# Attention decode step with a gated MLP on one core: the last head group's softmax between its predecessor's value chunks, the output projection around the last values, and one MLP weight in two transfers

## The chip, the core and the metric

The kernel runs on one core of a Trainium2 chip. The core has a matrix engine (TensorE, PE in the profile), a vector engine (VectorE, DVE), a scalar engine (ScalarE, ACT), GpSimd (POOL) and SyncE (SP), which here only issues transfers from HBM to the on-chip memory. Each engine runs its own queue of instructions in order, and the engines wait for one another and for transfers through semaphores. The metric is the device time of one execution in microseconds (us). The time before is the median of three runs.

## What is computed

One token of a pre-norm transformer block: attention against a cache of 4096 positions with 32 heads of 128, then a gated MLP with a tanh GELU. All inputs are bf16.

```python
def _A_ref(x, k_cache, v_cache, wq, wo):      # 32 heads, each with its own K and V
    q = (x @ wq).reshape(B, Sq, Hq, Dh)...
    scores = jnp.einsum("bhqd,bhkd->bhqk", q, k) * (Dh ** -0.5)
    p = _softmax(scores, axis=-1)
    o = jnp.einsum("bhqk,bhkd->bhqd", p, v)
    return o.reshape(B, Sq, Hq * Dh) @ wo

def _B_ref(x, w_gate, w_up, w_down):          # 640 -> 1728 -> 640
    h = _gelu(x @ w_gate) * (x @ w_up)
    return h @ w_down

h = x + _A_ref(_layernorm(x), k_cache, v_cache, wq, wo)
out = h + _B_ref(_layernorm(h), w_gate, w_up, w_down)
```

K and V are 32 MB each, and all that is read comes to 84 MB.

## The kernel before

The 32 heads are worked in 8 groups of 4 (`NG = 8`, numbered 0 to 7). A group's K and V fill one buffer each, of which there are two (`kbuf`, `vbuf`), so group g can be loaded when group g - 2 is done with its buffer. Partitions hold head and position: 32 partitions for each head, 128 positions in each partition.

The order of the instructions on each engine is written out by hand: a small scheduler class records each operation with the operations that it waits for, in program order, and each engine executes its own in that order. So a step that is written earlier stands earlier in the queue of its engine, and an operation that waits holds up all that stands behind it on its engine.

For one group the steps are small functions, and the loop over n interleaves those of three groups:

- `mult` (DVE, L321): K times the query, in four pieces; `fold` (PE, L330): eight matmuls with the identity for each piece, which add up parts of each product; `red` (DVE, L337): the rest of the sum, giving the scores.
- `top` (DVE, L345): the maximum of each partition. `turn` (PE, L349): these maxima turned into one row. `head` (DVE, L354): one maximum for each head. `soft` (PE L359, then ACT L362 and L366): the maximum spread to all partitions, and four exponentials, one for each head.
- `values` (PE, L377): 32 matmuls of 512 columns, in four chunks of 8. The first three chunks of group n - 1 stand in iteration n, the last in iteration n + 1. For the last group `values_last` (L385) does the same with 128 matmuls of 4 columns, with V as the stationary operand.
- `extract` (DVE, L391 and L394) and `column` (PE, L399): a group's result taken out of the accumulator and turned into a column for each head.

Every two groups (a quarter w of the heads, 8 heads) are finished together: `total` (PE, L403) and `invert` (DVE, L425) give the reciprocal sums of the softmax, `spread` (DVE, L410 and L412), `gather` (PE, L417) and `place` (DVE, L421) scale the result and put it into the form that the output projection reads. `project` (PE, L551) multiplies one quarter with its part of wo, in 40 matmuls of one column each.

After the loop there is a tail. Before the change it stands in this order: the last group's last reduction, `top`, `place` of quarter 2, `turn`, `head`, the last value chunk of group 6, `soft`, `extract` and `column` of group 6, `total` and `invert` of quarter 3; then `project` of quarters 0, 1 and 2; then the last group's values; then `spread`, `gather`, `place` and `project` of quarter 3. The residual and the layer norm follow (L563 to L286), then 70 matmuls with w_gate and 70 with w_up (`up`, L591), the GELU and its product with the up part (DVE, the last step `hm` in L607), a small matmul for the uneven remainder (L609), 56 matmuls with w_down (L623), a copy (L627) and the store (L628).

All large transfers are issued by SP in one queue. Behind the loop these are: wo's first three quarters, the last V in two parts (the first three quarters of the positions, then the last), wo's last quarter, w_gate, w_up, and w_down in four parts (80, 1280, 640 and 160 KB). w_gate and w_up are written over the two K buffers, w_down over a V buffer, wo over wq. So w_up waits for the last `mult`, and w_down for the last value chunk of group 6. w_gate and w_up have five slices each (`c` in `up`), and each slice's 14 matmuls wait for the transfer that brings it.

Of the kernel before, what the change touches and what calls it, by code (L numbers as in the profile page):

```python
# [23 lines left out]
NG = H // HG  # L24
# [3 lines left out]
NP = R // RP  # L28
# [81 lines left out]
def bass_sequential_preLN__gqa_block_cached__glu_gated_geglu__decode_kernel(  # L110
# [129 lines left out]
    kfree, vfree = [None] * NG, [None] * NG  # L240
# [78 lines left out]
    def mult(g, s):  # L319
        n = g * NP + s  # L320
        return S.op("vector", lambda v: v.tensor_tensor(  # L321
            out=prod[n % NPR][:, :, :], in0=kbuf[g % 2][:, s * RP:(s + 1) * RP, :],
            in1=qb[:, g, :].unsqueeze(1).to_broadcast([128, RP, DH]), op=ALU.mult),
            [d_k[g], t_qb[g], fold_done.get(n - NPR)])

    def fold(g, s, t_mult):
        n = g * NP + s
        W = 512 // RP
        for j in range(DH // W):
            fold_done[n] = S.op("tensor", lambda t, j=j: t.matmul(  # L330
                pf[n % 2][:, :], Ibf[:, :], prod[n % NPR][:, :, j * W:(j + 1) * W],
                start=(j == 0), stop=(j == DH // W - 1)),
                [t_mult, t_ibf, red_done.get(n - 2)], token=(j == DH // W - 1))

    def red(g, s):
        n = g * NP + s
        red_done[n] = S.op("vector", lambda v: v.reduce_sum(  # L337
            sc[g % 2][:, s * RP:(s + 1) * RP],
            pf[n % 2][:, :].rearrange("p (r w) -> p r w", r=RP), axis=AX.X),
            [fold_done[n], t_exp[g - 2] if g >= 2 else None])  # L340
# [3 lines left out]
    def top(g):  # L344
        t_mx[g] = S.op("vector", lambda v: v.reduce_max(  # L345
            mx[:, g:g + 1], sc[g % 2][:, :], axis=AX.X), [red_done[g * NP + NP - 1]])

    def turn(g):
        t_mm[g] = S.op("tensor", lambda t: t.matmul(  # L349
            pm[0:1, 0:128], mx[:, g:g + 1], I32[:, :], start=True, stop=True),  # L350
            [t_mx[g], t_i32, t_exp[g - 1] if g else None])

    def head(g):
        t_mr[g] = S.op("vector", lambda v: v.reduce_max(  # L354
            mrow[0:1, g * HG:(g + 1) * HG],
            pm[0:1, 0:128].rearrange("p (h q) -> p h q", h=HG), axis=AX.X), [t_mm[g]])

    def soft(g):
        d = S.op("tensor", lambda t: t.matmul(  # L359
            pm[:, 256:256 + HG], ones[0:1, :], mrow[0:1, g * HG:(g + 1) * HG],  # L360
            start=True, stop=True), [t_mr[g]])
        e = S.op("scalar", lambda a: a.activation(  # L362
            nb[:, g * HG:(g + 1) * HG], pm[:, 256:256 + HG], ACTF.Copy, scale=-SCALE), [d])
        for hh in range(HG):
            lo, hi, h = hh * PPH, (hh + 1) * PPH, g * HG + hh
            t_exp[g] = S.op("scalar", lambda a, lo=lo, hi=hi, h=h, hh=hh: a.activation(  # L366
                P4[g % 2][lo:hi, :, hh], sc[g % 2][lo:hi, :], ACTF.Exp,
                bias=nb[lo:hi, h:h + 1], scale=SCALE, accum_out=RS[lo:hi, h:h + 1]),
                [e, t_p4[g % 2], t_rs, t_pv[g - 2] if g >= 2 else None])
# [3 lines left out]
    def values(g, lo, hi):  # L373
        for i in range(lo, hi):
            r = i * VR
            last = i == NV - 1
            t_pv[g] = S.op("tensor", lambda t, i=i, r=r, last=last: t.matmul(  # L377
                pv[g % 2][0:VM, :], P4[g % 2][:, r:r + VR, :], vbuf[g % 2][:, r:r + VR, :],
                start=(i == 0), stop=last),
                [t_exp[g], d_v[g][r], t_ext[g - 2] if g >= 2 else None], token=last)  # L380
        vfree[g] = t_pv[g]

    def values_last(g):
        for r in range(R):
            t_pv[g] = S.op("tensor", lambda t, r=r: t.matmul(  # L385
                pq[:, 0:HG], vbuf[g % 2][:, r, :], P4[g % 2][:, r, :],
                start=(r == 0), stop=(r == R - 1)),
                [t_exp[g], d_v[g][r], t_qb[NG - 1]], token=(r == R - 1))
# [9 lines left out]
    def column(g):  # L398
        t_acc[g] = S.op("tensor", lambda t: t.matmul(  # L399
            po[:, g * HG:(g + 1) * HG], xz[g % 2][:, :], hsel[:, :], start=True, stop=True), [t_ext[g]])  # L400

    def total(w):
        t_zz[0] = S.op("tensor", lambda t: t.matmul(  # L403
            pz[:, 0:HW], ones[:, :], RS[:, w * HW:(w + 1) * HW], start=True, stop=True),
            [t_exp[2 * w + 1], t_aP[w - 1] if w else None])

    def spread(w, src):
        for ps, lo, n, tok in src:
            h0 = w * HW + lo
            a = S.op("vector", lambda v, ps=ps, h0=h0, n=n: v.tensor_mul(  # L410
                aT[:, h0:h0 + n], ps, rz[:, h0:h0 + n]), [t_rz[w], tok])
        t_aL[0] = S.op("vector", lambda v: v.tensor_tensor(  # L412
            out=aL[:, :, :], in0=aT[:, w * HW:(w + 1) * HW].unsqueeze(2).to_broadcast([128, HW, DJ]),
            in1=jmask[:, :].unsqueeze(1).to_broadcast([128, HW, DJ]), op=ALU.mult), [a, t_jm, t_aP[w - 1] if w else None])
# [5 lines left out]
    def place(w, b):  # L420
        t_aP[w] = S.op("vector", lambda v: v.tensor_copy(  # L421
            aP[:, w * HW:(w + 1) * HW], pz[:, 16:16 + HW]), [b])

    def invert(w):
        t_rz[w] = S.op("vector", lambda v: v.reciprocal(  # L425
            rz[:, w * HW:(w + 1) * HW], pz[:, 0:HW]), [t_zz[0]])
# [7 lines left out]
    for n in range(NG):  # L434
        w = (n - 3) // 2 if n >= 3 and n % 2 else None
        p, o = n - 1, n - 2

        t_mul[0] = mult(n, 0)
        if p >= 0:
            red(p, NP - 1)  # L440
            top(p)
        if w is None and n >= 4:
            place((n - 4) // 2, t_g)
        t_mul[1] = mult(n, 1)

        fold(n, 0, t_mul[0])
        if p >= 0:
            turn(p)
            head(p)
        if o >= 0:  # L450
            values(o, 3 * CH, NV)
        fold(n, 1, t_mul[1])
        red(n, 0)
        t_mul[2] = mult(n, 2)
        if p >= 0:
            soft(p)
        if w is not None:
            total(w)
        if 2 <= n + 1 < NG:
            t_qlast = query(n + 1)  # L460
        fold(n, 2, t_mul[2])
        red(n, 1)
        if w is not None:
            invert(w)
        if o >= 0:
            extract(o)
        t_mul[3] = kfree[n] = mult(n, 3)
        if o >= 0:
            column(o)
        if p >= 0:  # L470
            values(p, 0, CH)
        fold(n, 3, t_mul[3])
        red(n, 2)
        if w is not None:
            spread(w, [(po[:, w * HW:(w + 1) * HW], 0, HW, t_acc[o])])
        if p >= 0:
            values(p, CH, 2 * CH)
        if w is not None:
            t_g = gather(w)
        if p >= 0:  # L480
            values(p, 2 * CH, 3 * CH)

        if n == 0:
            load_k(2)
            load_v(1)
        else:
            if 2 <= n < NG - 1:
                load_v(n)
            if n + 2 < NG:
                load_k(n + 2)  # L490


    g = NG - 1
    w = NW - 1


    red(g, NP - 1)
    top(g)
    place(w - 1, t_g)
    turn(g)  # L500
    head(g)
    values(g - 1, 3 * CH, NV)
    soft(g)
    extract(g - 1)
    column(g - 1)
    total(w)
    invert(w)

    def pieces(slot, dst, src, cuts, waits):
        toks = []  # L510
# [7 lines left out]
    def load_wo(lo, hi):  # L518
# [8 lines left out]
    d_wg = pieces("wg", wg_sb, B_w_gate[:, :].rearrange("(p c) n -> p c n", c=NC_D),  # L527
                  [0, 5], [kfree[NG - 2]])
    d_wu = pieces("wu", wu_sb, B_w_up[:, :].rearrange("(p c) n -> p c n", c=NC_D),
                  [0, 5], [kfree[NG - 1]])  # L530
    d_wdr = S.dma("sync", "wdr", lambda s: s.dma_start(
        wd_sb[:, NFT, 0:D // 2], B_w_down[NFT * 128:DF, :].rearrange("r (h n) -> (r h) n", h=2)), [vfree[NG - 2]])
    d_wd = []
# [11 lines left out]
    def project(w):  # L545
        tok = None
        for c in range(HW):
            for cc in range(NC_D):
                last = w == NW - 1 and c == HW - 1 and cc == NC_D - 1
                first = w == 0 and c == 0 and cc == 0  # L550
                tok = S.op("tensor", lambda t, c=c, cc=cc, first=first, last=last: t.matmul(  # L551
                    pp[:, cc:cc + 1], wo_sb[:, w, c, cc::NC_D], aP[:, w * HW + c:w * HW + c + 1],
                    start=first, stop=last, skip_group_check=True),
                    [t_aP[w], d_wo[w], red_done[NG * NP - 2]], token=last)
        return tok

    for i in range(w):
        project(i)
    values_last(g)
    spread(w, [(po[:, w * HW:w * HW + HG], 0, HG, t_acc[NG - 2]), (pq[:, 0:HG], HG, HG, t_pv[NG - 1])])  # L560
    place(w, gather(w))
    b = project(w)
# [99 lines left out]
```

## Time and profile before

| | |
|---|---|
| median of 3 runs | 205.08 us (204.92 to 206.71) |
| the profiled execution | 206.38 us, of which the span from the first to the last instruction is 205.1 us |
| granted TensorE clock, mean over the span | 0.907 |
| PE busy | 158.6 us (77%), 1069 matmuls |
| DVE busy | 116.8 us (57%) |
| ACT busy | 30.4 us (15%) |
| read from HBM | 84.23 MB, 411 GB/s over the span |

The profile is one execution on the chip. Busy times are shares of the span; transfers and engines run beside one another, so the shares do not add up. In the chain of waits and in the timeline each line has the start, the length, the engine and the line of the program, all in us from the first instruction. The time from issue to landing of a transfer includes its wait in the queue behind the ones before it.

### The profile page before, as it was taken

The page shows a single profiled execution, that of the slowest core. Times are in us where ns is not written, and L with a number is a line of the kernel's source. Part 1 is how long each engine was busy: PE and PEld are TensorE (multiplying, and loading weights), DVE is VectorE, ACT ScalarE, POOL GpSimd, SP SyncE. Part 2 cuts the span into 40 slices and gives each one's busy share as a digit, 9 for nine tenths or more (in the row PEclk, how much of TensorE's full clock was granted, in tenths as well). Part 3 has the DMA queues.
Part 4 walks back from the last instruction along what each step waited for, and adds up shares of the span by engine and source line. Part 5 has one row for each costly group of instructions (what it writes and reads, how often), then busy time and mean ns, then how long its engine had stood idle before and what let it go on. Part 6 is the DMA issues. An engine that isn't in the chain of part 4 may idle for free.

```text
span 205.1 us, 2478 instructions
## 1 busy us (share of the span) xinstructions
PE 158.6 (77%) x1069; PEld 73.7 (36%) x1075; DVE 116.8 (57%) x152; ACT 30.4 (15%) x110; POOL 1.2 (1%) x7
## 2 busy tenths in 40 slices
PE   0002759679869968998999499999986999597595
PEld 0001113233324322443343124334422434397494
DVE  4004087997099538875991777599719782401221
ACT  2000210006003200330060004102400130400000
POOL 1000000000000000000000000000000000000000
PEclk9999999999999996999999759999997899965555
DMA  7999999999999999999999999999999999999980
GB/s 256 407 455 409 415 460 454 409 415 447 457 409 422 428 474 409 412 417 466 434 415 422 434 457 415 415 422 460 441 412 422 402 423 454 402 431 428 412 329 0
DMA packets 4162, 84.38 MB, mean 411 GB/s; under 512 B 568, under 2 KB 824, under 8 KB 952
## 3 DMA queue, kind: packets, MB, share of 16 engines
q1 hardware_dynamic: 4008, 84.23, 96.2%
q8 instruction: 8, 0.13, 0.3%
q10 hardware_dynamic: 144, 0.00, 0.0%
q14 instruction: 2, 0.02, 0.0%
HBM read 84.23 MB, written 0.00 MB: 411 GB/s over the span
## 4 chain that ended last, share of the span: by engine, by line
DMA 43%; PE 31%; DVE 19%; ACT 4%; issue 2%; DVEq 0%
DMA kbuf<-in_A_k_cache_dram 36%; DVE prod L321 13%; PE pf L330 10%; DMA x_sb<-in_A_x_dram 8%; PE pu L377 4%; PE pg L377 4%; PE pf L551 3%; DVE sc L337 3%; PE pq L300 2%; ACT P L366 2%; PE pq L385 2%; PE pg L591 2%; PE pu L591 2%; DVE xz L394 1%; PE pf L623 1%
## 5 line engine op out<-in xcount | busy, mean ns | idle before, releaser
L321 DVE TENSOR_TENSOR prod<-kbuf,qb 128x4096 bf16<-128x4096 bf16 x32 | 72.8, 2279 | 36.6 <-DMA kbuf<-in_A_k_cache_dram 30.4
L330 PE MATMUL pf<-prod,Ibf 128*128 128x512 bf16 x256 | 66.7, 408 | 17.2 <-DVE prod L321 17.2
L330 PEld LDWEIGHTS pf<-prod,Ibf 128*128 128x128 bf16 x256 | 24.4, 103 | 56.4 <-DVE prod L321 23.7
L377 PE MATMUL pg<-vbuf,P 128*16 128x512 bf16 x128 | 30.1, 379 | 0.1
L337 DVE TENSOR_REDUCE sc<-pf 128x32 f32<-128x512 f32 x32 | 21.7, 678 | 6.2 <-PE pf L330 6.2
L377 PE MATMUL pu<-vbuf,P 128*16 128x512 bf16 x96 | 24.5, 407 | 0.0
L362 ACT ACTIVATE nb<-pm 128x4 f32<-128x4 f32 x8 | 1.4, 173 | 123.9 <-PE pm L359 123.9
L366 ACT ACTIVATE P<-sc,nb 32x128 bf16<-32x128 f32 x32 | 18.5, 578 | 0.9
L377 PEld LDWEIGHTS pg<-vbuf,P 128*16 128x16 bf16 x128 | 10.6, 89 | 14.9 <-issue 1.7
L272 PE MATMUL pz<-st,ones 128*128 128x2 f32 x4 | 1.2, 364 | 17.6 <-DVE st L271 17.6
L300 PE MATMUL pq<-wq_sb,xb 128*128 128x512 bf16 x34 | 10.8, 452 | 4.2 <-DVE xb L286 2.2
L377 PEld LDWEIGHTS pu<-vbuf,P 128*16 128x16 bf16 x96 | 8.8, 96 | 13.5 <-issue 4.5
L306 ACT CAST qb<-pq 32x128 bf16<-32x128 f32 x32 | 8.2, 256 | 6.5 <-PE pq L300 5.8
L366 ACT ACTIVATION_READ_ACCUMULATOR P<-sc,nb 32x1 f32 x32 | 8.0, 251 | 0.0
L551 PE MATMUL pf<-aP,wo_sb 128*128 128x1 bf16 x160 | 6.8, 178 | 1.1 <-issue 0.8
L289 DVE CAST x<-x_sb 128x5 f32<-128x5 bf16 x1 | 0.2, 172 | 12.9 <-DMA x_sb<-in_A_x_dram 12.9
L272 PEld LDWEIGHTS pz<-st,ones 128*128 128x128 f32 x4 | 1.0, 313 | 17.6 <-DVE st L271 17.6
L394 DVE TENSOR_REDUCE xz<-xm 16x128 f32<-16x512 f32 x7 | 7.2, 1023 | 0.2
L551 PEld LDWEIGHTS pf<-aP,wo_sb 128*128 128x128 bf16 x160 | 6.7, 131 | 1.2 <-issue 0.8
L300 PEld LDWEIGHTS pq<-wq_sb,xb 128*128 128x128 bf16 x40 | 3.8, 111 | 8.2 <-DVE xb L286 2.3
L283 ACT ACTIVATE ln<-ln 128x1 f32<-128x1 f32 x2 | 0.4, 202 | 30.7 <-DVE ln L281 30.7
L410 DVE TENSOR_TENSOR aT<-pq,rz 128x4 bf16<-128x4 f32 x1 | 0.2, 161 | 8.0 <-PE pq L385 8.0
(77 smaller groups left out, 69.4 us busy)
## 6 DMA issues: line engine op xcount, KB each, us to landing
kbuf<-in_A_k_cache_dram SPq DMA_DIRECT2D x8, 4096.0 KB, 25.2
vbuf<-in_A_v_cache_dram SPq DMA_DIRECT2D x7, 4096.0 KB, 22.7
wq_sb<-in_A_wq_dram SPq DMA_DIRECT2D x1, 5120.0 KB, 15.3
wo_sb<-in_A_wo_dram SPq DMA_DIRECT2D x1, 3840.0 KB, 28.4
vbuf<-in_A_v_cache_dram SPq DMA_DIRECT2D x1, 3072.0 KB, 18.3
wg_sb<-in_B_w_gate_dram SPq DMA_DIRECT2D x1, 2160.0 KB, 27.7
wu_sb<-in_B_w_up_dram SPq DMA_DIRECT2D x1, 2160.0 KB, 27.7
wo_sb<-in_A_wo_dram SPq DMA_DIRECT2D x1, 1280.0 KB, 23.0
```

Source lines behind the costliest of these rows:

```text
L272: c = S.op("tensor", lambda t: t.matmul(ps[:, 0:2], ones[:, :], st[:, o:o + 2], start=True, stop=True), [b, t_one])
L300: tok = S.op("tensor", lambda t, c=c, n0=n0: t.matmul(pq[:, :], xb[:, c, :], wq_sb[:, c, n0:n0 + HG * DH], start=(c == 0), stop=(c == NC_D ...
L306: t_qb[g] = S.op("scalar", lambda a, lo=lo, hi=hi, hh=hh: a.copy(qb[lo:hi, g, :], pq[lo:hi, hh * DH:(hh + 1) * DH]), [tok])
L321: return S.op("vector", lambda v: v.tensor_tensor(out=prod[n % NPR][:, :, :], in0=kbuf[g % 2][:, s * RP:(s + 1) * RP, :], in1=qb[:, g, :]. ...
L330: fold_done[n] = S.op("tensor", lambda t, j=j: t.matmul(pf[n % 2][:, :], Ibf[:, :], prod[n % NPR][:, :, j * W:(j + 1) * W], start=(j == 0) ...
L337: red_done[n] = S.op("vector", lambda v: v.reduce_sum(sc[g % 2][:, s * RP:(s + 1) * RP], pf[n % 2][:, :].rearrange("p (r w) -> p r w", r=R ...
L366: t_exp[g] = S.op("scalar", lambda a, lo=lo, hi=hi, h=h, hh=hh: a.activation(P4[g % 2][lo:hi, :, hh], sc[g % 2][lo:hi, :], ACTF.Exp, bias= ...
L377: t_pv[g] = S.op("tensor", lambda t, i=i, r=r, last=last: t.matmul(pv[g % 2][0:VM, :], P4[g % 2][:, r:r + VR, :], vbuf[g % 2][:, r:r + VR, :],
L385: t_pv[g] = S.op("tensor", lambda t, r=r: t.matmul(pq[:, 0:HG], vbuf[g % 2][:, r, :], P4[g % 2][:, r, :], start=(r == 0), stop=(r == R - 1 ...
L394: t_ext[g] = S.op("vector", lambda v: v.reduce_sum(xz[g % 2][:, :], xm[:, :, :].rearrange("p r d -> p d r"), axis=AX.X), [a, t_acc[g - 2] ...
L551: tok = S.op("tensor", lambda t, c=c, cc=cc, first=first, last=last: t.matmul(pp[:, cc:cc + 1], wo_sb[:, w, c, cc::NC_D], aP[:, w * HW + c ...
L591: b = S.op("tensor", lambda t, s=s, c=c, part=part, first=first, last=last: t.matmul(ps[:, s:s + 1], part, hln[:, c:c + 1], start=first, s ...
```

## The change

There are three edits, all near the end of the program.

1. The last group's last `red`, its `top`, `turn` and `head` stand in the loop's last iteration, between the second and the third value chunk of group 6, ahead of `gather` of quarter 2. `soft` of the last group stands ahead of the fourth chunk, and `place` of quarter 2 behind `head`.
2. `project` of quarters 0 and 1 comes directly behind the fourth chunk; `column` of group 6 and `total` and `invert` of quarter 3 come behind these projections; then the last group's values, and behind them `project` of quarter 2. Then `spread`, `gather`, `place` and `project` of quarter 3 as before.
3. w_up is loaded in two transfers, slices 0 to 2 (1296 KB) and slices 3 and 4 (864 KB), with a semaphore each.

No instruction is added or removed on PE, DVE and ACT; SP has one transfer more.

```diff
             spread(w, [(po[:, w * HW:(w + 1) * HW], 0, HW, t_acc[o])])
         if p >= 0:
             values(p, CH, 2 * CH)
+        if n == NG - 1:
+            red(n, NP - 1)
+            top(n)
+            turn(n)
+            head(n)
         if w is not None:
             t_g = gather(w)
...
-    red(g, NP - 1)
-    top(g)
     place(w - 1, t_g)
-    turn(g)
-    head(g)
+    soft(g)
     values(g - 1, 3 * CH, NV)
-    soft(g)
     extract(g - 1)
-    column(g - 1)
-    total(w)
-    invert(w)
...
     d_wu = pieces("wu", wu_sb, B_w_up[:, :].rearrange("(p c) n -> p c n", c=NC_D),
-                  [0, 5], [kfree[NG - 1]])
+                  [0, 3, 5], [kfree[NG - 1]])
...
-    for i in range(w):
+    for i in range(w - 1):
         project(i)
+    column(g - 1)
+    total(w)
+    invert(w)
     values_last(g)
+    project(w - 1)
     spread(w, [(po[:, w * HW:w * HW + HG], 0, HG, t_acc[NG - 2]), (pq[:, 0:HG], HG, HG, t_pv[NG - 1])])
     place(w, gather(w))
     b = project(w)
```

## The prediction

> **What bounds the kernel now.** I read the page first (busy shares, slices, transfers), then the chain of waits, then the timeline from 158 us, because the edits touch nothing earlier. The chain, in order of time (start, us, what):
>
> ```profile
> 175.27 0.32 PE pm L359 x2
> 175.59 0.02 issue
> ...
> 178.26 0.39 PE pz L403 x2
> 178.65 4.78 PE pf L551 x120
> 183.43 0.86 PE pq L385 x32
> ...
> 188.09 1.36 PE pf L551 x30
> 189.45 0.80 issue
> 190.25 0.54 PE pf L551 x10
> ...
> 193.57 3.58 PE pg L591 x70
> 197.15 3.43 PE pu L591 x70
> ...
> 201.09 2.00 PE pf L623 x30
> ```
>
> From 175.59 the tail is a serial run on PE: a hole to 178.26 while ACT makes the last exponentials, 120 projections, the last values, 40 more projections, the layer norm, gate, up, down. No wait in it ends with a transfer. But the transfers run just ahead of it. Their issues in the timeline, and the time from issue to landing in the list of transfers:
>
> ```profile
> 161.02 0.81 SPq L252 DMA_DIRECT2D vbuf<-in_A_v_cache_dram  x2
> ...
> 161.88 0.43 SPq L519 DMA_DIRECT2D wo_sb<-in_A_wo_dram  x1
> ...
> 162.36 0.43 SPq L513 DMA_DIRECT2D wg_sb<-in_B_w_gate_dram  x1
> ...
> 167.53 0.33 SPq L513 DMA_DIRECT2D wu_sb<-in_B_w_up_dram  x1
> ...
> 175.67 1.38 SPq L536 DMA_DIRECT2D wd_sb<-in_B_w_down_dram  x3
> ```
> ```profile
> wg_sb<-in_B_w_gate_dram SPq DMA_DIRECT2D x1, 2160.0 KB, 27.7
> wu_sb<-in_B_w_up_dram SPq DMA_DIRECT2D x1, 2160.0 KB, 27.7
> wo_sb<-in_A_wo_dram SPq DMA_DIRECT2D x1, 1280.0 KB, 23.0
> wd_sb<-in_B_w_down_dram SPq DMA_DIRECT2D x1, 1280.0 KB, 22.8
> ...
> wd_sb<-in_B_w_down_dram SPq DMA_DIRECT2D x1, 640.0 KB, 23.9
> wd_sb<-in_B_w_down_dram SPq DMA_DIRECT2D x1, 160.0 KB, 23.8
> ```
>
> Issue plus landing: last values 179.32 and 181.80 (the second issue at 161.40, with 20.4 us), last quarter of wo 184.88, w_gate 190.06, w_up 195.23; w_down's three issues lie 0.475 apart, so 198.47, 200.04, 200.42. All go through one queue and the 16 DMA engines are 9 tenths busy until 200. So there are two limits: PE's tail, now 203.08, and the last w_down landing, 200.42, which no edit of PE's order moves. What the change can win is the distance between them, less the matmuls that must follow the landing.
>
> **The change, part by part, on the clock of this profile.**
>
> *Softmax between the value chunks.* The last reduction and `top` end on DVE at 170.61 already (L345: 170.32 + 0.29), but `turn` stood behind another chunk and ran at 173.32. Now it follows chunk 2 (end 171.39): 0.22, gather 0.11, chunk 3 1.82, so `soft` starts at 173.54 and the exponentials end at 173.86 + 0.20 + 4 x 0.605 = 176.5 instead of 178.22. PE blocks at `turn` if the maximum is late (gather and chunk 3 queue behind): slack 0.78. It blocks at `soft` if `head` is late (chunk 4 queues behind): `head` ends near 171.9, slack 1.6. Both free; if that cover were gone, each late us is a us on PE. `place` now stands behind `head` on DVE; only the projection of quarter 2 reads it, 11 us later. Chunk 4 ends 0.32 later, at 175.59, behind `soft`; `extract` and the w_down issues, which wait for that chunk, start 0.32 later. The issues are covered by 20 us of queued transfers (w_up lands at 195.2); without that cover they would cost 0.32.
>
> *Projections into the hole.* From 175.59 PE runs 80 projections at 4.78/120 = 0.0398: 178.78. `column` and `total` (0.38 + 0.39) to 179.55; what they need (xz at 177.4, exponentials at 176.5) is there, and `invert` follows on DVE beside the values. The last values take 187.07 - 183.43 = 3.64, to 183.19. Their data: 179.32 is just in time, and matmul 97 starts near 182.28, after 181.80. So the last values end 3.88 earlier than before.
>
> *Quarter 2 behind the values.* 40 x 0.0398 = 1.59, to 184.78. `spread` beside it needs 187.64 - 187.07 = 0.57, so 1.02 of the 1.59 is on the path: the gather queues behind it on PE. Gather to `place` 188.09 - 187.64 = 0.45: 185.23; wo's last quarter (184.88) is there. The last 40 take 1.36 + 0.54 = 1.90, plus a gap like the one at 189.45. That gap waits for no semaphore; I read it as instruction supply, because the instruction queue moves a packet in the window just before it (187.8 to 189.1):
>
> ```profile
> q1 hardware_dynamic: 38, 0.54, 99.1%
> q8 instruction: 1, 0.02, 5.1%
> ```
>
> Bounds 0 and 0.80; I take 0.80, the only row. The projection ends at 187.13 to 187.93 against 190.79, 2.9 to 3.7 earlier. Adding 193.57 - 190.79 = 2.78 for residual and layer norm gives 189.91 to 190.71. Here w_gate (190.06) becomes late by up to 0.15.
>
> *Gate and up.* Gate 3.58, to 193.64 or 194.29. Unsplit, `up` would now wait for 195.23. Split, 1296 KB and 864 KB land apart. Price of the extra transfer: 2160 KB took 195.23 - 190.06 = 5.17 (428 GB/s); the 640 KB piece took 1.57 (417 GB/s). At 417 the two parts take 5.30, so the split costs 0 to 0.13; a gain is excluded, as no smaller row is clearly quicker. I take 0.07, the middle. SP has one issue more, 0.33 to 0.43, inside the 7.7 us it then idles. Part 1 lands at 195.30 - 2.1 = 193.2, before gate ends. Its 42 matmuls at 3.43/70 = 0.049 end at 195.7 to 196.35; 28 more at 197.1 to 197.7; up to the multiply and the small matmul 201.02 - 200.58 = 0.44, so `down` could start at 197.5 to 198.2.
>
> *The end.* Now w_down sets it, each landing 0.07 later. 36 matmuls from 198.54 + 0.05 at 0.032 (201.02 to 202.17 for 36) end their starts at 199.75; 16 wait for 200.11 + 0.05, to 200.67; the last 4 start up to 200.77 and end 0.34 later: 201.11. Before: 203.08. Gain **1.97** (1.91 at the dear split, 2.04 at the free one). PE's own path (198.2 + 2.06 = 200.3) leaves 0.85 of slack, so the 0.80 gap changes nothing.
>
> The profiled execution took 206.38 (span 205.1 and 1.28 around it), so 204.4; the median of 205.08 becomes **203.1**.
>
> **Two rules against the rows.** The row on splitting is 417 beside 428 GB/s. The Trainium skill, "DMA: Bandwidth & Descriptors", section "Rules for kernel authors", asks for at least 1 MiB per DMA, and 864 KB is under it; its section "Anatomy of one DMA" states a fixed cost of about 2.0 us per DMA on the GpSimd path. Were that paid on a full queue, every w_down landing would slip by 2.0 and the gain would be about 0; no run here shows such a cost, and the 640 and 160 KB pieces, landing 1.57 and 0.38 after their predecessors, speak against it.
>
> The granted clock falls to 0.50 at about 180.6, while PE is full of projections, and stays there. The projections do not notice, 53 in 2.10 us and then 69 in 2.60 (columns: PE busy, PEclk):
>
> ```profile
> 178.50:180.60 2.10, 2.09 (x53) 1.00 0.99 415
> 180.70:183.30 2.60, 2.60 (x69) 0.50 1.07 442
> ```
>
> The Trainium skill, "TensorE: Matmul & The Clock Gate", section "HAM oscillation", says to leave no idle gap over some 3.4 us; filling the hole might then keep the full clock. By that rule the matmuls behind the last landings would halve their spacing and the gain would be about 2.3; by the row, where the clock fell during busy projections, it stays 1.97.
>
> **The rivals.**
> A. *Transfers set the end*, as above: 202.8 to 203.3. For it: every landing is in the table and PE's path has 0.85 to spare. 58%.
> B. *PE still sets the end*, because gaps grow: the same instructions are consumed closer together. About 2,144 PE instructions on 8 instruction packets is 268 each, so 175.6 to 187 (586 instructions) asks for two or three. If another two gaps of 0.80 appear, PE's path is 200.3 + 1.6 = 201.9, gain 1.2; with three 0.4. 203.2 to 204.7. 20%.
> C. *More than the floor*: w_down lands 0.3 to 0.6 sooner than in this profile, or the last matmuls run closer together. PE's own path would allow it (200.3, so a gain up to 2.8): gain 2.3 to 2.6, 202.5 to 202.8. 10%.
> D. *Nothing comes of it*: the landings behind the split slip by about what PE gains, 1.5 to 2.0. Against it the 417 GB/s of the 640 KB piece. 204.7 to 205.4. 4%.
> E. *Slower, by instruction supply.* If every packet in this stretch costs the whole time from request to use (packet seen from 187.8, PE resumed 190.25: 2.45), three cost 7.35 in place of 0: the projection ends at 187.13 + 7.35 = 194.5, 3.7 later than before, so 208.8. It decides from a sum of gaps of 3.66 (187.13 to 190.79), 1.2 each. Against it: the same dense stretch of 120 projections and 128 values before held no gap. 8%.
>
> **How the numbers follow.** A measurement tells about 1%, 2.05 us, from no change. A lies astride it (203.03): I give 0.32 of its 0.58 to faster, for C's effects may share in it. Faster 0.32 + 0.10 = 0.42; slower 0.08; the same 0.50. The range runs from C (202.5) through most of B (204.4); outside lie E, D and B's end, nearly 2 in 10. A alone: 202.8 to 203.3.
>
> **What would show it.** Right: exponentials end by 176.6, PE has no hole after 175.6, the last values end near 183.2, the last wo projection near 187 to 188, `up` waits for a w_up transfer, `down` ends in waits for w_down, PE ends 0.6 after the last landing. Wrong: the last w_down landing moved by over 0.3, the value matmuls wait for their data, gaps over 1 us without a releaser among the projections, or `hm` later than 199.

## The result, and the profile after

| | before | after |
|---|---|---|
| median, 16 runs each | 205.19 us (204.73 to 208.32) | 204.24 us (204.02 to 204.61) |
| the profiled execution | 206.38 us, span 205.1 | 204.25 us, span 203.0 |
| granted clock, mean | 0.907 | 0.924 |

The ratio is 0.9934, with a 95% interval of 0.9911 to 0.9957; it leaves out the two executions of before (208.11 and 208.32 us) that were in a slower state. The median falls by 0.95 us, the profiled execution by 2.13. The forecast was 1.97 for both. So on the profile's clock the sum was right within 0.2, and it is the step to the median that has to be explained.

The chain of waits of the kernel after, from the end of the fourth value chunk (start, us, what; its line numbers are up to two off those of before, so L549 is `project` and L593 is `up`):

```profile
175.43 3.29 PE pf L549 x80
178.72 0.31 PE po L399 x2
179.03 0.52 PE pz L403 x2
179.55 1.91 PE pq L385 x72
181.46 0.57 issue
182.03 1.65 PE pq L385 x56
183.69 1.60 PE pf L549 x40
...
185.57 1.36 PE pf L549 x30
186.93 1.28 issue
188.21 0.54 PE pf L549 x10
...
191.53 3.54 PE pg L593 x70
195.07 3.39 PE pu L593 x70
...
198.97 1.99 PE pf L625 x30
```

The hole that stood at 175.59 is filled: projections start when the fourth chunk ends. The last values begin at 179.55, as worked out. But there are now two pieces called "issue", in which PE waits for nothing that the profile shows: 0.57 inside the last values and 1.28 behind 30 of the last 40 projections. Before, the same two places had 0.06 and 0.80. PE ends at 200.97; the last w_down landing is at 200.2, 0.2 earlier than before.

w_up came in two pieces, and the second in time. The issue, and the time to landing of its two parts, from the list of transfers:

```profile
167.28 0.80 SPq L511 DMA_DIRECT2D wu_sb<-in_B_w_up_dram  x2
```
```profile
wu_sb<-in_B_w_up_dram SPq DMA_DIRECT2D x1, 1296.0 KB, 25.6
...
wu_sb<-in_B_w_up_dram SPq DMA_DIRECT2D x1, 864.0 KB, 27.3
```

Part 1 is there at 192.9 and part 2 near 195.0, while gate ends at 195.07.

### The profile page after: what moved, and what is told of

It is laid out like the page before. It is cut to its first block, busy times and chain, and to the rows that moved or that the text cites. A ratio compares the mean times of both kernels' runs of the same rounds, so it can differ in the third digit from the quotient of the medians.

```text
span 203.0 us, 2479 instructions
## 1 busy us (share of the span) xinstructions
PE 154.9 (76%) x1069; PEld 72.9 (36%) x1075; DVE 116.6 (57%) x152; ACT 30.5 (15%) x110; POOL 1.2 (1%) x7
## 4 chain that ended last, share of the span: by engine, by line
DMA 46%; DVE 25%; PE 23%; ACT 2%; issue 2%; DVEq 0%
DMA kbuf<-in_A_k_cache_dram 38%; DVE prod L321 17%; DMA x_sb<-in_A_x_dram 8%; PE pf L330 5%; DVE sc L337 4%; PE pg L377 4%; PE pf L549 3%; PE pq L300 2%; PE pq L385 2%; PE pg L593 2%; PE pu L593 2%; ACT P L366 1%; DVE xz L394 1%; PE pf L625 1%; PE pu L377 1%
## 5 line engine op out<-in xcount | busy, mean ns | idle before, releaser
L330 PE MATMUL pf<-prod,Ibf 128*128 128x512 bf16 x256 | 65.6, 404 | 20.6 <-DVE prod L321 20.6
L377 PE MATMUL pu<-vbuf,P 128*16 128x512 bf16 x96 | 22.2, 379 | 0.0
L377 PEld LDWEIGHTS pu<-vbuf,P 128*16 128x16 bf16 x96 | 8.1, 89 | 11.3 <-issue 1.3
L549 PE MATMUL pf<-aP,wo_sb 128*128 128x1 bf16 x160 | 7.0, 178 | 1.5 <-issue 1.3
L549 PEld LDWEIGHTS pf<-aP,wo_sb 128*128 128x128 bf16 x160 | 6.7, 131 | 2.1 <-issue 1.8
L391 DVE TENSOR_TENSOR xm<-pg,rmask 16x512 f32<-16x512 f32 x4 | 2.7, 671 | 3.7 <-PE pg L377 3.7
```

The costliest lines, as they stand in the source:

```text
L330: fold_done[n] = S.op("tensor", lambda t, j=j: t.matmul(pf[n % 2][:, :], Ibf[:, :], prod[n % NPR][:, :, j * W:(j + 1) * W], start=(j == 0) ...
L391: a = S.op("vector", lambda v: v.tensor_tensor(out=xm[:, :, :], in0=pv[g % 2][0:VM, :].rearrange("p (r d) -> p r d", r=VR), in1=rmask[:, : ...
```

## The experiments

Two theories stood at the start. *Theory 1:* the profiled execution of before was longer than a typical one, because the granted clock was 0.50 right behind PE's wait for the last K; and the kernel after is held by the last w_down landings, so it cannot gain what a typical execution has already. *Theory 2:* the gaps without a releaser, read as instruction supply (PE stands because its next instructions have not arrived), grew and ate the gain. A third question is which of the three edits brings what.

**before_again**: before, unchanged, one more profile.

> The kernel before, unchanged, profiled once more. Theory 1 (the clock): the profiled execution of before was not a typical one; its 206.38 us contain about 1.3 us for a granted clock of 0.50 between 156.7 and 160.2, right behind PE's wait for the last K, and an execution near 205.0 has full clock there and its last value chunk of group 6 ends near 174.0 instead of 175.3. If this execution takes over 206 instead, it shows the 0.50 stretch again. Theory 2 (instruction supply): executions near 205.0 and near 206.4 have the same times up to 175.3 and differ behind it, in the gaps without a releaser.

Measured: 205.65 us. The windows of before's first profile, and below them the same windows of this one (us, PE busy, PEclk, DMA share, GB/s):

```profile
153.00:156.70 3.70, 1.28 (x6) 1.00 0.99 425
156.80:160.10 3.30, 3.30 (x10) 0.50 1.04 447
```
```profile
153.00:156.70 3.70, 2.28 (x11) 1.00 1.03 443
156.80:160.10 3.30, 3.30 (x17) 1.00 0.92 397
```

In the first execution PE stood idle for 2.55 us before the last group's first `fold` (152.87 to 155.42) and then ran 10 matmuls at half clock; here its work before the wait ended 1 us later, it stood for 1.42 us, and it ran 17 at full clock in the same 3.30 us. The kernel after's own profile has the fall too: it stood for 2.92 us, and the clock is 0.78 and 0.74 in the same two windows. The chain of this execution:

```profile
173.47 0.32 PE pm L359 x2
...
177.07 4.78 PE pf L551 x120
181.84 0.85 PE pq L385 x32
182.70 0.38 issue
183.07 2.74 PE pq L385 x96
...
188.19 1.35 issue
189.54 0.54 PE pf L551 x10
```

`soft` runs at 173.47 instead of 175.27, 1.8 earlier. But the gaps are 0.38 + 1.35 = 1.73 instead of 0.86, so half of the lead is lost again, and the multiply `hm` is only 0.74 earlier (199.93 against 200.67). Both theories hold a part.

**before_warm** and **after_warm**: the same addition to both kernels, so that PE is busy in that wait.

```diff
+    def warm(k):
+        for i in range(k):
+            S.op("tensor", lambda t: t.matmul(
+                pz[:, 64:448], Ibf[:, :], qb[:, 0:3, :], start=True, stop=True), ...)
...
+        if n == NG - 1:
+            warm(12)
         fold(n, 0, t_mul[0])
```

> Before, with 12 matmuls of 384 columns added on PE in front of the last group's first fold, into unused columns of a PSUM bank, so that PE is busy while it waits for the last K. Nothing is left out. Theory 1: the clock stays at 1.0 between 153 and 164, the last value chunk of group 6 ends near 174.0, and the time is 204.7 to 205.1 in every execution, none at 206 or above; span about 203.7. Theory 2: the time is that of before, 204.7 to 208 with the same spread, and the gap without a releaser in the last 40 projections stays, 12 matmuls earlier (behind 18 instead of 30), since 24 instructions are added.

> The changed kernel with the same 12 matmuls added. Nothing is left out. Theory 1: PE's tail starts 1.0 to 1.5 us earlier, but the last landing of w_down stays near 200.2 and PE can end no sooner than about 0.5 us behind it, so the time falls only 0.2 to 0.4, to 203.9 to 204.1, and the gain over before_warm stays at about 1.0. Theory 2: gaps without a releaser set the end, so it falls by as much as the tail starts earlier, 1.0 or more, to 203.2 or below. Both gaps (0.57 in the last values, 1.28 in the last 40 projections) should come 12 matmuls earlier if they are instruction supply.

before_warm measured 205.67 us (204.88 to 206.1, 10 runs), beside 205.62 (204.70 to 208.50, 25 runs) for before, taken alongside. Theory 1 had it at 204.7 to 205.1 in every execution, and that failed. What it had right is the upper end: without the two longest (207.99 and 208.50), 10 of 23 executions of before took over 206.1, none of the ten of before_warm did, and in its profile the clock is 1.00 through the windows above. The rest went into the gaps, 0.57 and 1.55. They came behind 20 of the last values and behind 18 of the last projections, instead of 32 and 30 before: 12 matmuls earlier, for 12 matmuls added. A gap that moves with the count of instructions, and not with the step it stood in, speaks for instruction supply.

after_warm measured 204.22 us, the kernel after 204.24; theory 1 had it at 203.9 to 204.1, theory 2 at 203.2 or below, so both asked for too much, theory 2 by 1.0. Its tail on PE starts 1.5 us earlier (the first projection at 173.90 against 175.36) and nothing is gained, because it now waits for transfers: first 1.42 us for the last V, which takes nearly all of the lead, then for wo and for w_down. From its timeline (start, us, ..., in brackets the idle time before and what ended it):

```profile
179.30 3.57 PE L385 MATMUL pq<-P,vbuf 128*128 128x4 bf16 x128 [1.42 <-DMA vbuf<-in_A_v_cache_dram]
...
184.95 0.85 PE L557 MATMUL pf<-aP,wo_sb 128*128 128x1 bf16 x18 [0.45 <-DMA wo_sb<-in_A_wo_dram]
186.21 1.01 PE L557 MATMUL pf<-aP,wo_sb 128*128 128x1 bf16 x22 [0.40 <-issue]
...
198.47 1.24 PE L633 MATMUL pf<-wd_sb,hm 128*1 128x160 bf16 x32 [0.93 <-DMA wd_sb<-in_B_w_down_dram]
199.49 0.35 PE L633 MATMUL pf<-wd_sb,hr 128*1 128x160 bf16 x4
200.02 0.84 PE L633 MATMUL pf<-wd_sb,hm 128*1 128x160 bf16 x20 [0.18 <-DMA wd_sb<-in_B_w_down_dram]
```

The last 20 matmuls start 0.05 behind a landing at 199.97, which the chain of this execution gives as the release. That is the floor; the kernel after, in its own profile, ends 0.1 above it by PE.

**after_warm_nodown** and **before_nodown**: the four w_down transfers left out; `down` reads wo's tile in their place, so the output is no longer the block's.

```diff
-    d_wdr = S.dma("sync", "wdr", ...)
-    for i, n in enumerate(WD_PARTS): ...
+    d_wd = [d_wo[NW - 1]] * NF
...
-        return hm[:, s:s + 1], wd_sb[:, s, j * NQ:(j + 1) * NQ]
+        return hm[:, s:s + 1], wo_sb[:, 1, s % HW, j * NQ:(j + 1) * NQ]
```

> after_warm without the four w_down transfers, the down matmuls reading wo's tile. Theory 1: after_warm waits for w_down's landings; in its profile the multiply ended at 197.3 and the down matmuls could start there instead of at 198.47 and 200.02, so the time falls by 1.2 to 1.5, to 202.7 to 203.0. Theory 2 (gaps of instruction supply set the end): it stays within 0.3 of after_warm, 203.9 to 204.5.

> Before without the four w_down transfers (2.16 MB, some 5 us of the queue); the down matmuls read wo's tile in their place, so the output is not the reference's and the computation is the same in number and shape. Theory 1: before is bound by PE's tail, so the time is that of before, at most 0.3 less. Rival (the last landings bind before as well): 1 us less or more.

Measured: after_warm_nodown 203.08 us (202.94 to 203.19, 4 runs), 1.14 under after_warm and just above the expected 202.7 to 203.0, and its `down` starts at 197.82 without a wait. before_nodown 206.87 us (204.87 to 208.10), against before a ratio of 1.0031 (0.9986 to 1.0077): nothing gained. So w_down's landings hold the kernel after once PE's tail is early, and they do not hold before.

**after_whole**: the kernel after with w_up in one transfer (`[0, 3, 5]` back to `[0, 5]`).

> The changed kernel with w_up in one transfer as before. Theory: gate ends at 195.07 in the profile of after and the second part of w_up landed at 194.97, so the split buys nothing in that execution: the same within 0.15 us. In executions where PE's tail is about 1.3 us earlier, up waits for the whole w_up, to about 195, and the time is at most 0.2 longer. The rival, that the extra transfer costs: 0.1 faster or more with the last landing 0.07 or more earlier.

Measured: 204.55 us (204.43 to 204.80), 0.3 above the kernel after, more than was expected of any execution. In the chain `up` is released by w_up:

```profile
167.49 27.66 DMA wu_sb<-in_B_w_up_dram
195.16 0.05 issue
195.20 3.56 PE pu L593 x70
```

`up` starts 0.13 later than in the kernel after (195.20 against 195.07) and, starting from a standstill, shows 3.56 instead of 3.39. The split is worth 0.3. Its price is not to be seen: one whole w_up lands 5.2 us behind w_gate, and in two parts as well.

**soft_only**: the first edit alone. **order_only**: the second alone. **order_split**: the second and third.

> Before with the first edit alone: the last group's reduction, maxima and exponentials between the value chunks, all else as before, nothing left out. Theory 1 (the projections fill the hole, the transfers cap the gain): the exponentials end 1.7 us earlier, but column then waits for extract, which ends 1.8 us behind the fourth chunk, so total ends only about 0.5 us earlier; the time is that of before or up to 0.5 less. Rival (the earlier softmax is what brings the gain): the whole 1.0 to 1.4 us gain of the change is there, 204.2 to 204.5.

> Before with the second edit alone: quarters 0 and 1 of the projection behind the fourth chunk, quarter 2 behind the last values; softmax late as before, w_up in one transfer, nothing left out. Theory 1: the exponentials end about 2.7 us behind the fourth chunk and the 80 projections take 3.3 us, so nothing waits for them: the time is that of after_whole, 204.4 to 204.7, and PE has no hole behind the fourth chunk. Rival (the earlier softmax brings the gain): 205 or more.

> The second and third edit without the first: projections around the last values and w_up in two parts, the softmax of the last group late as before. Nothing is left out. Theory 1: the time of the changed kernel, 204.1 to 204.4; the first edit is worth nothing beside the second. Rival (the first edit brings part of the gain): 0.2 or more above.

Measured: soft_only 205.78 us, a ratio of 0.9991 (0.9951 to 1.0032): no gain that stands out, though the interval leaves room for some 0.5 us. order_only 204.54, the same as after_whole. order_split 204.20 (204.07 to 205.17), the same as the kernel after. That w_down's landings hold both does not hide a gain here: in order_split, too, PE goes from the 80 projections to `column` (178.74) and `total` (179.05) without a wait. So the early softmax is worth nothing beside the others, and nothing that can be measured alone. The timeline of soft_only shows why:

```profile
173.72 1.89 PE L377 MATMUL pg<-vbuf,P 128*16 128x512 bf16 x8
177.43 0.38 PE L399 MATMUL po<-hsel,xz 16*128 16x4 f32 x2 [1.81 <-DVE xz L394]
177.74 0.39 PE L403 MATMUL pz<-RS,ones 128*128 128x8 f32 x2
```

`total` no longer waits for the exponentials, but `column` in front of it still waits for `extract`, which cannot start before the fourth chunk ends. One wait of 1.81 remains of a hole of about 2.7, and 0.5 us is what `total` gains.

**after_noload** and **before_noload**: no transfer behind wo's last quarter; gate, `up` and `down` read wo's tile in place of their weights.

```diff
-    d_wg = pieces("wg", ...)
-    d_wu = pieces("wu", ...)
+    d_wg = d_wu = [d_wo[NW - 1]] * NC_D
+    d_wd = [d_wo[NW - 1]] * NF
...
-                part = w[:, c, DF - 128:DF]
+                part = flat(c)[:, DF - 128:DF]     # flat(c): a row of wo's tile
```

> The changed kernel without the transfers of w_gate, w_up and w_down; the matmuls of gate, up and down read wo's tile in their place, the same in number and shape, so the output is not the reference's. The queue is then empty from about 184.8 on. If the gaps without a releaser are instruction supply behind queued data: the gap inside the last values, whose packet is asked for while the queue is full, stays at 0.2 to 0.6; the gap behind 30 of the last 40 projections (0.8 to 1.6 in eight profiles) falls under 0.3, because its packet no longer waits; its packet starts by 185 and not at 185.7 or later. If the gaps have another cause on PE: the second stays at 0.8 or more.

> Before without the transfers of w_gate, w_up and w_down, the matmuls reading wo's tile. As for after_noload: by instruction supply the gap behind 30 of the last 40 projections (0.80 to 1.35 before) falls under 0.3, since its packet starts behind 184.9, when the queue is empty; by another cause it stays. The time falls by about the gap, to 204.0 to 205.7 depending on the clock in the wait for the last K, and not by the 7 us of queue that are left out.

Measured, one execution each: 202.15 us and 203.64 us. From the timeline of after_noload, the last values, quarter 2 and quarter 3 of the projection:

```profile
179.43 3.55 PE L385 MATMUL pq<-P,vbuf 128*128 128x4 bf16 x128
182.85 1.74 PE L536 MATMUL pf<-aP,wo_sb 128*128 128x1 bf16 x40
...
184.88 1.76 PE L536 MATMUL pf<-aP,wo_sb 128*128 128x1 bf16 x40 [0.26 <-DVE aP L421]
```

No gap is left: 40 projections in one run of 1.76, where the kernel after needed 1.36 + 1.28 + 0.54. In before_noload both are gone as well, and that is why it fell under the 204.0 that was expected. The packet for the second gap was moved between 182.5 and 183.7, in the kernel after between 185.6 and 186.8 (after_noload, then the kernel after; packets, MB, share of the 16 DMA engines in the window):

```profile
q1 hardware_dynamic: 35, 0.26, 50.8%
q8 instruction: 1, 0.02, 5.3%
```
```profile
q1 hardware_dynamic: 30, 0.52, 103.6%
q8 instruction: 1, 0.02, 5.3%
```

The first gap was expected to stay and did not; since it varies between 0 and 0.57 in profiles with a full queue, one execution does not settle that half.

## Why the prediction came out as it did

The range of 202.5 to 204.4 held the 204.24, and "the same" had the largest chance, 0.50. In part that was luck: the upper end of the range stood for rival B's longer gaps, which cost the end of the kernel some 0.1 us, while what moved the time from 203.1 to 204.24 was a step that no rival named. Point by point:

- *"204.4; the median of 205.08 becomes 203.1"* is the step that failed. 204.4 against 204.25 for the profiled execution is right; the median should have been the same number. Case A says that transfers set the end: that is a time on the clock, the last landing plus what follows it, and it does not fall because the execution of before that it is compared with was a shorter one. The profiled execution of before lay 1.2 above the median of the 16 runs, and the same 1.97 was taken off both. Before, executions spread over 2.3 us in the first comparison (204.73 to 206.98); the profiles of before differ by the clock behind the wait for the last K and by the length of two gaps. After, they spread over 0.6, because the floor takes up both. So the gain depends on where before happens to lie: beside order_split's 204.20, 13 executions of before had a median of 206.83, a distance of 2.6 us in place of 0.95. What the split between clock and gaps is in an execution of before that was not profiled stays open: before_warm removed the clock's part and its median did not move.
- *The softmax edit,* for which the sum takes nothing off: right, shown by order_split. That `column`, not the exponentials, is the next wait was in the sum only as "xz at 177.4"; soft_only shows that it is what remains.
- *80 projections in the hole:* right, 179.40 to 179.55 against 179.55. It is most of the second edit's gain. The rest is the 0.57 that PE stood for `spread` before (187.07 to 187.64): `spread` now runs beside quarter 2, and the gather follows at 185.28 without a wait. order_only has both.
- *"Bounds 0 and 0.80; I take 0.80":* mis-sized. The kernel after has 0.57 + 1.28 = 1.85, and other profiles with the same order of the tail up to 1.57 in one gap. The projection ended at 188.75 and not between 187.13 and 187.93. The slack of 0.85 that was to absorb such a thing was just used up: PE ends at 200.97 in the profile, by PE, where 201.11 by the landings was predicted. Rival B's mechanism was there, at the price of the slack, and 204.24 lies in B's interval and not in A's, but by the step to the median and not by B's gaps. Of the signs of being wrong one came, a gap of over 1 us without a releaser among the projections.
- *The split at 0 to 0.13:* the lower end is right. Its gain was larger than the 0.1 that the sum implies: 0.3. The rule of at least 1 MiB per DMA (the Trainium skill, "DMA: Bandwidth & Descriptors", "Rules for kernel authors") did not bind here: the 864 KB part costs nothing that can be seen.
- *The clock:* the fall to 0.50 in the tail came again, at about 179.0 in the kernel after, with PE at work from 155.2 on (0.26 us idle in all). Filling the hole did not keep the full clock, so the row was right. The rule (the Trainium skill, "TensorE: Matmul & The Clock Gate", "HAM oscillation": no idle gap over some 3.4 us) was kept, and the clock fell all the same; the hole that was filled, 2.7 us, was shorter than that already. In the wait for the last K the clock fell behind shorter idle times than the rule names: in the eight of the thirteen profiles in which PE stood for 2.55 to 3.15 us there. It stayed at 1.00 in the five with 0.86 to 1.42 us, three of them filled with the 12 matmuls. The length alone does not decide it: in before_again PE stood for 2.93 us at 113.5 and the clock stayed at 1.00.
- *"`up` waits for a w_up transfer"* did not come true in the profile after, since gate was late by the gaps. It did in after_whole and order_only.

No version tried that computes the same beats the kernel after by more than the measurement can tell; after_warm reaches the same floor.

## What to carry to other kernels

When a change takes the end from an engine to the transfers, work out the new time as an absolute one, last landing plus what must follow it, and compare it with the median of before; the gain found on one profiled execution is not a number to subtract from another. Before that, ask why the profiled execution differs from the median: here 1.2 us, more than the 0.95 by which the median fell. And where two waits end close together, removing one alone is worth only the distance to the other.

## What the runs showed of the hardware that was not expected

The trace's instruction queue brings 8 packets of 16 KB (0.13 MB) in one execution, counted on the same 16 DMA engines as the data, and the gaps tie those in the tail to PE. With the data queue full, PE resumed 2.3 to 2.6 us after the start of a packet that it stood waiting for, and the packets in the dense tail began 5.9 to 6.5 us apart (in the profiles of before, before_again and after). With no data queued behind wo, two began 3.7 us apart (182.6 and 186.3 in after_noload) and neither gap was there. A stretch of short matmuls (128 values in 3.6 us, 256 instructions with their weight loads) uses up instructions faster than that, since 2144 on 8 packets make some 268 to a packet, so a dense tail behind a full queue is partly bound by its instruction count.
